# Third exp added ahead of the softmax sums, first adds on GpSimd, values and feed-forward one score burst later

## The chip, the cores and the metric

The kernel runs on one core of one Trainium2 chip. The metric is the device time of one execution in microseconds (us), as the median of several executions. Executions carry a state, fast or slow. All kernels of one group of runs ran on the same chip beside runs of the kernel before. A ratio below is the mean time of one kernel's fast runs over that of the kernel before's fast runs of the same rounds, so it is not quite the ratio of the medians that are quoted.

In this text TensorE is the matmul engine (PE in the profile, PEld its weight loads), VectorE is DVE, ScalarE is ACT, GpSimd is POOL.

## The reference

Grouped-query attention (batch 8, 16 query heads, 4 key and value heads, 384 positions, 64 wide), then a gated feed-forward with a spatial mix:

```python
scores = scale * q @ k.T ; attn = exp(scores - max) ; attn /= sum(attn) ; x = attn @ v
h = max(x @ w_in, 0) ; u, v = halves of h
v_n = (v - mean(v)) / sqrt(var(v) + 1e-6)
v_s = w_spatial @ v_n + b_spatial
out = (u * v_s) @ w_out
```

The kernel computes it per batch in f16 with f32 sums. It takes no maximum before the exp, which the size of the inputs allows.

## The kernel before: what matters

Every step is a small function, and a text lists the steps in the order in which they are issued. Each engine takes its own instructions from that text in that order; nothing overtakes on an engine. A step waits by semaphore for the data and buffers that it needs. A quote mark on a step means the batch before, two mean the one before that.

A batch has 18 score units: two groups of heads (gp), three chunks of 512 columns (c), three key tiles (t). The unit number u runs over t fastest. A "visit" is one burst of three units on TensorE (`s`), their three exps on ScalarE (`e`), and filler work for TensorE.

```python
def expo(b, u):      # ScalarE: aT[t] of 128x1024 f16 from two PSUM banks
    nc.scalar.activation(T["aT", b, gp][:, t, :, c*512:(c+1)*512], banks[...], AF.Exp, scale=scale)

def add(b, gp, c):   # "a": sT = aT[0] + aT[1], VectorE
    nc.vector.tensor_tensor(T["sT", b, gp][:, :, cs], aT[:, 0, :, cs], aT[:, 1, :, cs], ALU.add)

def add2(b, gp, c):  # "f": sT += aT[2]; in the file, but unused before
    T["all", b, gp] = True
    nc.vector.tensor_tensor(sT, sT, T["aT", b, gp][:, 2, :, cs], ALU.add)

def sums(b, gp, quad):  # "m": row sums by matmul with ones; one pass over each part
    parts = [aT[:, t] for t in range(NST)] if sT is None else [sT] if ("all", b, gp) in T else [sT, aT[:, 2]]
    tiles(f32(x, S), quad, [(ones32, a) for a in parts])
# "r": 1/sum by Ln and Exp on ScalarE; "x": values on TensorE; "n": xT = values * 1/sum on VectorE (PSUM in)
# "V": gate_v on TensorE and v_r = max(.,0) on VectorE; "S": bn_stats; "rs": rstd on ScalarE
def v_norm(b, engine):  # "vn": three of these, f32 in SBUF to f16 in SBUF
    engine.tensor_scalar(v_n, T["v_r", b, st], mv[:, st, 0:1], rstd[:, st:st+1], op0=ALU.subtract, op1=ALU.mult)
# "p": spatial, "U": gate_u, "O": project and an osb copy out of PSUM on VectorE ("Oc": in 32-column tiles)

C1 = "m10' m11' r10' r11' x100' n100' ... n111'"      # sums and values of group 1 of the batch before
C0 = "m00 m01 r00 r01 x000 n000 ... n011"
VISITS = [
    "s0 s1 s2 e0 e1 e2 a12' Oc0'' Oc1'' lk+ lq0+ lv+ lq1+", C1,
    "s3 s4 s5 e3 e4 e5 V0' S0' V1' S1' a00 a01 ck+ cq0+",
    "s6 s7 s8 e6 e7 e8 V2' S2' O2'' O3'' tk+ tq0+ cq1+ cv+",
    "s9 s10 s11 e9 rs' e10 e11 a02 Oc4'' Oc5'' vn' tq1+", C0,
    "s12 s13 s14 e12 e13 e14 p0' U0' p1' U1' a10",
    "s15 s16 s17 e15 e16 e17 p2' U2' p3' U3' a11",
]
```

The steps `ck cq cv` are casts of k, q and v on GpSimd. `banks` are the eight PSUM banks; a helper gives out the bank that was used longest ago. A score burst of three units takes six of them.

The softmax here doesn't subtract the row's maximum and nothing guards it: scores larger than these inputs give would overflow.

## Time and profile before

| | before |
|---|---|
| median of 3 runs | 256.83 us (256.55 to 256.88) |
| profiled span | 255.2 us |
| steady state | one batch every 28.8 us |

The page's first part gives each engine's busy time and share of the span:

```profile
PE 242.1 (95%) x2545; PEld 117.2 (46%) x2545; DVE 186.5 (73%) x348; ACT 172.1 (67%) x228; POOL 57.9 (23%) x100
```

TensorE is the busiest by far. A table of stretches shows one steady period. Its columns are the stretch, its length, then busy time of PE, PEld, DVE, ACT and POOL with their instruction counts, the granted TensorE clock, the DMA share and GB/s:

```profile
109.85:138.65 28.80, 28.43 (x307) 13.41 (x306) 22.24 (x40) 21.23 (x28) 6.85 (x10) 1.00 0.68 173
```

TensorE is busy 28.43 of 28.80 us at full clock. VectorE has 6.6 us to spare and GpSimd 22.

The timeline of another period (start, length, engine, line, operation; in brackets the idle time before it and what ended it) shows the work that the change removes, and a place where TensorE waits:

```profile
141.13 0.34 PE L331 MATMUL banks<-sT,ones 128*32 128x384 f16 x4
141.29 0.34 PE L331 MATMUL banks<-aT,ones 128*32 128x384 f16 x4
...
152.47 0.82 PE L309 MATMUL banks<-qT,kT 64*128 64x512 f16 x5
152.79 1.27 DVE L513 COPY osb<-banks 128x512 f32<-128x512 f32 x2
153.51 0.37 PE L309 MATMUL banks<-qT,kT 64*128 64x512 f16 x1 [0.22 <-DVE osb L513]
...
156.38 1.45 DVE L460 TENSOR_SCALAR v_n<-v_r,mv,rstd 128x512 f16<-128x512 f32 x3
```

The first two lines are the two-part sums. The next three show the last matmul of a score burst waiting for an osb copy to free its bank.

### The profile page before, as it was taken

The page shows a single profiled execution, that of the slowest core. Times are in us where ns is not written, and L with a number is a line of the kernel's source. Part 1 is how long each engine was busy: PE and PEld are TensorE (multiplying, and loading weights), DVE is VectorE, ACT ScalarE, POOL GpSimd, SP SyncE. Part 2 cuts the span into 40 slices and gives each one's busy share as a digit, 9 for nine tenths or more (in the row PEclk, how much of TensorE's full clock was granted, in tenths as well). Part 3 has the DMA queues.
Part 4 walks back from the last instruction along what each step waited for, and adds up shares of the span by engine and source line. Part 5 has one row for each costly group of instructions (what it writes and reads, how often), then busy time and mean ns, then how long its engine had stood idle before and what let it go on. Part 6 is the DMA issues. An engine that isn't in the chain of part 4 may idle for free.

```text
span 255.2 us, 6119 instructions
## 1 busy us (share of the span) xinstructions
PE 242.1 (95%) x2545; PEld 117.2 (46%) x2545; DVE 186.5 (73%) x348; ACT 172.1 (67%) x228; POOL 57.9 (23%) x100
## 2 busy tenths in 40 slices
PE   5899998979999999999999999999999999999993
PEld 5342434443454534553454434553354534554671
DVE  1544579987977599577976599577986599587953
ACT  3799799876766958776776958776776959730000
POOL 1717921624400054003700053002800000000000
PEclk9589999999999999999999999999999999999998
DMA  6999999959590688719591687519591204010424
GB/s 177 272 245 333 168 172 225 252 138 314 184 236 0 196 256 139 185 51 302 184 216 28 187 266 200 122 39 308 189 217 25 85 0 167 3 71 13 164 82 168
DMA packets 57228, 41.98 MB, mean 165 GB/s; under 512 B 26352, under 2 KB 53360, under 8 KB 57200
## 3 DMA queue, kind: packets, MB, share of 16 engines
q1 hardware_dynamic: 54208, 38.31, 55.9%
q0 software_dynamic: 2848, 3.15, 8.0%
q8 instruction: 20, 0.33, 0.5%
q10 hardware_dynamic: 144, 0.13, 0.1%
q14 instruction: 8, 0.07, 0.1%
HBM read 25.95 MB, written 12.58 MB: 151 GB/s over the span
## 4 chain that ended last, share of the span: by engine, by line
PE 57%; DVE 19%; DMA 12%; POOL 5%; SPq 3%; issue 3%; ACT 0%
PE banks L119 43%; DMA q<-in_q_dram 8%; PE banks L331 7%; PE banks L309 7%; DVE osb L513 4%; DVE sT L344 3%; DVE bn L449 3%; DVE v_n L460 3%; DVE v_r L436 3%; DVE xT L391 3%; DMA v<-in_v_dram 2%; POOL w_in L142 2%; DMA qT<-q 2%; POOL q L232 2%; SPq L210 1%
## 5 line engine op out<-in xcount | busy, mean ns | idle before, releaser
L321 ACT ACTIVATE aT<-banks 128x1024 f16<-128x1024 f32 x144 | 137.7, 1023 | 49.3 <-PE banks L309 48.4
L309 PE MATMUL banks<-qT,kT 64*128 64x512 f16 x288 | 47.0, 393 | 4.8 <-DMA qT<-q 1.5
L119 PE MATMUL banks<-xT,w_in 128*128 128x384 f16 (+1 forms) x320 | 47.2, 294 | 0.6 <-DVE v_r L438 0.6
L119 PE MATMUL banks<-w_out,gT 128*32 128x512 f16 (+2 forms) x508 | 45.4, 378 | 0.0
L119 PE MATMUL banks<-w_in,xT 128*128 128x512 f16 x192 | 44.7, 380 | 0.0
L391 DVE TENSOR_TENSOR xT<-banks,rec 128x384 f16<-128x384 f32 x64 | 31.4, 549 | 11.3 <-ACT rec L364 9.6
L232 POOL CAST q<-q 128x384 f16<-128x384 f32 x56 | 31.5, 594 | 16.2 <-DMA q<-in_q_dram 12.6
L119 PEld LDWEIGHTS <-w_in 128*128 128x128 f16 x320 | 27.3, 98 | 15.8 <-issue 1.4
L331 PE MATMUL banks<-aT,v 128*32 128x384 f16 x768 | 34.4, 326 | 0.0
L513 DVE COPY osb<-banks 128x512 f32<-128x512 f32 x47 | 31.2, 684 | 3.5 <-PE banks L119 3.4
L119 PEld LDWEIGHTS <-gT 128*32 128x32 f16 (+1 forms) x508 | 18.8, 96 | 27.1 <-issue 8.8
L189 POOL CAST k<-k 128x768 f16<-128x768 f32 x7 | 5.8, 829 | 104.2 <-DMA k<-in_k_dram 94.9
L119 PEld LDWEIGHTS <-xT 128*128 128x128 f16 x192 | 17.2, 98 | 25.6 <-issue 7.4
L344 DVE TENSOR_TENSOR sT<-aT 128x1024 f16<-128x1024 f16 x39 | 27.7, 738 | 0.0
L493 DVE SCALAR_TENSOR_TENSOR gT<-banks,vs 128x384 f16<-128x384 f32 x24 | 13.4, 558 | 17.0 <-PE banks L119 17.0
L331 PEld LDWEIGHTS <-v 128*32 128x32 f16 x768 | 20.3, 97 | 11.1 <-issue 0.8
L309 PEld LDWEIGHTS <-kT 64*128 64x128 f16 x288 | 11.2, 94 | 28.5 <-issue 22.3
L436 DVE TENSOR_SCALAR v_r<-banks 128x512 f32<-128x512 f32 x21 | 14.4, 688 | 11.8 <-PE banks L119 11.1
L119 PE MATMUL banks<-wsT,v_n 128*128 128x384 f16 x96 | 20.8, 327 | 0.8
L362 ACT ACTIVATE rec<-banks 128x384 f32<-128x384 f32 x32 | 15.6, 488 | 4.1 <-PE banks L331 4.0
L480 DVE TENSOR_TENSOR vs<-banks,bias_tp 128x384 f32<-128x384 f32 x28 | 15.6, 556 | 2.8 <-PE banks L119 2.8
L364 ACT ACTIVATE rec<-rec 128x384 f32<-128x384 f32 x32 | 16.7, 523 | 1.0
(49 smaller groups left out, 141.3 us busy)
## 6 DMA issues: line engine op xcount, KB each, us to landing
q<-in_q_dram SPq DMA_DIRECT2D x31, 384.0 KB, 6.9
out_dram<-osb SPq DMA_DIRECT2D x22, 512.0 KB, 3.2
v<-in_v_dram SPq DMA_DIRECT2D x8, 384.0 KB, 6.3
k<-in_k_dram SPq DMA_DIRECT2D x7, 384.0 KB, 5.7
w_in<-in_moe_w_in_dram POOLq DMA_DIRECT2D x16, 128.0 KB, 6.0
w_out<-in_moe_w_out_dram POOLq DMA_DIRECT2D x2, 512.0 KB, 9.3
out_dram<-osb SPq DMA_DIRECT2D x3, 256.0 KB, 2.0
ws<-in_moe_w_spatial_dram SPq DMA_DIRECT2D x1, 576.0 KB, 10.2
```

Of the source, the lines that this page charges most:

```text
L119: nc.tensor.matmul(dst[c : c + cols], w[:, c : c + cols], m, start=(i == 0), stop=(i == n - 1))
L232: engine(T["q16", b, gp][:, 2 * qd : 2 * qd + 2, :, half, :], T["q32", b, gp][:, qd, 2 * half : 2 * half + 2, :].rearrange("p j (t d) -> p ...
L309: nc.tensor.matmul(banks[:, xs[half], :], T["kT", b][lo:hi, t, gp, :], rhs[lo:hi, c * 512 : (c + 1) * 512], start=True, stop=True,)
L321: nc.scalar.activation(T["aT", b, gp][:, t, :, c * 512 : (c + 1) * 512], banks[:, x : y + 1 : y - x, :], AF.Exp, scale=scale)
L331: nc.tensor.matmul(dst[32 * i : 32 * (i + 1), :], weights if len(weights.shape) == 2 else weights[:, half, :], a[:, half, j * S : (j + 1) ...
L344: nc.vector.tensor_tensor(T["sT", b, gp][:, :, cs], aT[:, 0, :, cs], aT[:, 1, :, cs], ALU.add)
L362: nc.scalar.activation(rec, f32(x, S), AF.Ln)
L364: nc.scalar.activation(rec, rec, AF.Exp, scale=-1.0)
L391: nc.vector.tensor_tensor(T["xT", b][:, gp * 4 + quad * 2 + jj, :], f32(x, S), T["rec", b, gp, quad], ALU.mult)
L436: nc.vector.tensor_scalar(v_r, banks[:, x, :], 0.0, None, op0=ALU.max)
L480: nc.vector.tensor_tensor(vs, f32(x, S), bias_tp, ALU.add)
L513: copy(osb[:, half * 512 : (half + 1) * 512], banks[:, x, :])
```

## The change

Its intent: TensorE sets the period, so take matmuls from it. If the third exp is added too, each sum reads one part instead of two. The first add of each chunk goes to the idle GpSimd. Of the six second adds of a batch, which are new, five go to VectorE and one (`fp10`) to GpSimd. Since a GpSimd add takes longer, everything that depends on it moves one score burst later.

```diff
-    def add(b, gp, c):
+    def add(b, gp, c, engine=nc.vector):
...
-        nc.vector.tensor_tensor(T["sT", b, gp][:, :, cs], aT[:, 0, :, cs], aT[:, 1, :, cs], ALU.add)
+        engine.tensor_tensor(T["sT", b, gp][:, :, cs], aT[:, 0, :, cs], aT[:, 1, :, cs], ALU.add)
... (add2 in the same way)
+        "ap": lambda b, gp, c: add(b, gp, c, nc.gpsimd), "fp": lambda b, gp, c: add2(b, gp, c, nc.gpsimd),
...
     VISITS = [
-        "s0 s1 s2 e0 e1 e2 a12' Oc0'' Oc1'' lk+ lq0+ lv+ lq1+", C1,
-        "s3 s4 s5 e3 e4 e5 V0' S0' V1' S1' a00 a01 ck+ cq0+",
-        "s6 s7 s8 e6 e7 e8 V2' S2' O2'' O3'' tk+ tq0+ cq1+ cv+",
-        "s9 s10 s11 e9 rs' e10 e11 a02 Oc4'' Oc5'' vn' tq1+", C0,
-        "s12 s13 s14 e12 e13 e14 p0' U0' p1' U1' a10",
-        "s15 s16 s17 e15 e16 e17 p2' U2' p3' U3' a11",
+        "s0 s1 s2 e0 e1 e2 ap12' f12' p2'' U2'' p3'' U3'' lk+ lq0+ lv+ lq1+",
+        "s3 s4 s5 e3 e4 e5 Oc0'' Oc1'' ap00 f00 ck+ cq0+", C1,
+        "s6 s7 s8 e6 e7 e8 V0' S0' V1' S1' ap01 f01 tk+ tq0+ cq1+ cv+",
+        "s9 s10 s11 e9 e10 e11 V2' S2' rs' O2'' O3'' ap02 f02 vn' tq1+",
+        "s12 s13 s14 e12 e13 e14 Oc4'' Oc5'' ap10", C0,
+        "s15 s16 s17 e15 e16 e17 p0' U0' p1' U1' ap11 fp10 f11",
     ]
+    SUBS = "ap12' f12'=>a12';ap01=>a01;ap02=>a02;Oc0'' Oc1''=>Oc2'';p2'' U2'' p3'' U3''=>O0'' O1'';O2'' O3''=>O3''"
+    SECOND = STEADY with SUBS applied          # (written as a loop)
...
-            play(b, STEADY)
+            play(b, STEADY if b > 2 else SECOND)
```

The last part of the text (after the last batch) is changed to match. Batches 0 and 1 keep their old steps; batch 2, called SECOND, is the way into the new order.

More of the change, by code (lines that the diff above doesn't have):

```diff
@@ L343, in add, with add2 @@
         cs = slice(c * 512, (c + 1) * 512)
-        nc.vector.tensor_tensor(T["sT", b, gp][:, :, cs], aT[:, 0, :, cs], aT[:, 1, :, cs], ALU.add)
-    def add2(b, gp, c):
+        engine.tensor_tensor(T["sT", b, gp][:, :, cs], aT[:, 0, :, cs], aT[:, 1, :, cs], ALU.add)
+    def add2(b, gp, c, engine=nc.vector):
         T["all", b, gp] = True
@@ L349, in add2 @@
         sT = T["sT", b, gp][:, :, cs]
-        nc.vector.tensor_tensor(sT, sT, T["aT", b, gp][:, 2, :, cs], ALU.add)
+        engine.tensor_tensor(sT, sT, T["aT", b, gp][:, 2, :, cs], ALU.add)
     def sums(b, gp, quad):
@@ L580 @@
     STEPS = {
-        "w": idle, "s": score, "e": expo, "m": sums, "a": add, "f": add2, "r": recip, "rd": recip_v, "x": value, "n": norm,
+        "w": idle, "s": score, "e": expo, "m": sums, "a": add, "f": add2,
+        "ap": lambda b, gp, c: add(b, gp, c, nc.gpsimd), "fp": lambda b, gp, c: add2(b, gp, c, nc.gpsimd),
+        "r": recip, "rd": recip_v, "x": value, "n": norm,
         "V": gate_v, "S": stats, "rs": rstd, "vn": lambda b: v_norm(b, nc.vector),
@@ L640 @@
     VISITS = [
-        "s0 s1 s2 e0 e1 e2 a12' Oc0'' Oc1'' lk+ lq0+ lv+ lq1+", C1,
-        "s3 s4 s5 e3 e4 e5 V0' S0' V1' S1' a00 a01 ck+ cq0+",
-        "s6 s7 s8 e6 e7 e8 V2' S2' O2'' O3'' tk+ tq0+ cq1+ cv+",
-        "s9 s10 s11 e9 rs' e10 e11 a02 Oc4'' Oc5'' vn' tq1+", C0,
-        "s12 s13 s14 e12 e13 e14 p0' U0' p1' U1' a10",
-        "s15 s16 s17 e15 e16 e17 p2' U2' p3' U3' a11",
+        "s0 s1 s2 e0 e1 e2 ap12' f12' p2'' U2'' p3'' U3'' lk+ lq0+ lv+ lq1+",
[4 more added lines that the diff above has]
+        "s15 s16 s17 e15 e16 e17 p0' U0' p1' U1' ap11 fp10 f11",
     ]
     STEADY = " ".join(VISITS)
+    SUBS = "ap12' f12'=>a12';ap01=>a01;ap02=>a02;Oc0'' Oc1''=>Oc2'';p2'' U2'' p3'' U3''=>O0'' O1'';O2'' O3''=>O3''"
+    SECOND = STEADY
+    for x in SUBS.split(";"):
+        SECOND = SECOND.replace(*x.split("=>"), 1)
     FIRST = """lk+ lq0+ lv+ lq1+
@@ L655 @@
     LAST = """
-        a12' Oc0'' Oc1'' m10' m11' r10' r11' x100' n100' x101' n101' x110' n110' x111' n111'
-        V0' S0' V1' S1' V2' S2' O2'' O3'' rs' vn' O4'' O5''
+        ap12' f12' p2'' U2'' p3'' U3'' Oc0'' Oc1'' m10' m11' r10' r11' x100' n100' x101' n101' x110' n110' x111' n111'
+        V0' S0' V1' S1' V2' S2' Oa2'' rs' vn' O3'' O4'' O5''
         pz0' pz1' pz2' pz3' Uz0' Uz1' O0' O1' Uz2' Oh2' Oh3' Oh4' Oz5'"""
```

## The prediction

> **What bounds the kernel now.** The page gives TensorE 95% of the span, VectorE 73%, ScalarE 67%, GpSimd 23%. The chain of waits shows a steady state that repeats every 28.8 us (score bursts at 105.48, 134.28, 163.02, 191.81 us). The stretch view of such a period has TensorE busy 28.4 of 28.8 us, VectorE 22, ScalarE 21, GpSimd 6.8, granted clock 1.00. So TensorE's own instructions set the period. In the timeline two places of it run longer than their work: the score burst at 152.47 us takes 1.34 us instead of the usual 0.75 (its last matmul waits for a VectorE copy "osb"), and the burst at 158.25 takes 1.03 (the next weight load waits for v_n and norms behind VectorE). That is about 0.87 us per period. The chain runs through VectorE from 148 to 159 us: v_r, bn, two sT adds, osb, v_n, xT.
>
> **What the change removes.** Each chunk's sums now read one tile (sT of all three exps) instead of two. The instruction order shows 184 "ones" matmuls instead of 280: 96 fewer, in 24 groups of four concurrent ones. In the timeline 16 of them take 0.65 us to the next group, 0.1625 us a group: 24 x 0.1625 = 3.9 us, 0.65 us per batch, in batches 2 to 7. All of it lies on TensorE and so on the critical path.
>
> **What it adds and moves.** VectorE: six first adds per batch (0.66 us alone, mean 0.738) become five second adds of the same shape, so slightly less. GpSimd: seven adds of 128x1024 f16 per batch. No trace has one yet. The Trainium skill, "GPSIMD Engine Reference", section "Elementwise — side-by-side cycle accounting", gives about 2.6 cycles an element for two inputs at 1.2 GHz: estimate 2.2 us each, 15.5 us a period, with casts about 22 of 28. It fits, and each has nearly a whole visit (4 to 6 us) between its exps and its reader. The skill's "SBUF — State Buffer", section "Who interferes with whom", says that two-input VectorE operations and GpSimd reads block each other; the trace agrees: sT adds lie between 657 and 1312 ns, the long ones during casts, and casts stretch from 510 to 1034 ns. By my timing of the visits second adds mostly run when GpSimd has just finished; I allow 1 to 3 us of blocking per period, on VectorE, which has 6 us of slack.
> Moving the values and the feed-forward one burst later takes two adds out of the crowded v_r stretch and moves v_n a burst ahead of its reader. I expect this to win back about 0.5 of the 0.87 us stall per period, 2.3 us over five periods. The ramp before 52 us is unchanged; the tail keeps its TensorE order and gains some tenths.
>
> **Prediction.** 256.8 - 3.9 - 2.3 + 0.3 for new waits: 250.9 us, eight in ten between 248.5 and 254.3. Faster by over 2%: 0.60; within 2%: 0.35; slower by over 2%: 0.05.
>
> **What would show it.** Period near 27.7 us; "ones" matmul busy about 7 us lower; GpSimd adds of 2.0 to 2.6 us and GpSimd busy near 150 us; no burst of over 1.1 us in steady state; VectorE second adds of 0.66 to 1.5 us.
>
> **What would make it wrong.** GpSimd adds of over 3 us: GpSimd then bounds the period, VectorE stands behind a late first add, and evacuations, banks and score bursts wait. Long mutual blocking: second adds of 2 us and more. Casts held behind adds, so transposes of q and k land after their burst. Or the stall only moves to another burst: then about 253 us.

## More of the kernel before

Experiments 1 to 4, 5 to 8 and 9 to 10 ran on three different chips; the kernel before had medians of 256.71, 256.73 and 256.88 us there.

From the table of groups (line, engine, operation, output and inputs, count, then total busy us and mean ns of one):

```profile
L344 DVE TENSOR_TENSOR sT<-aT 128x1024 f16<-128x1024 f16 x39 | 27.7, 738 | 0.0
L331 PE MATMUL banks<-aT,ones 128*32 128x384 f16 x176 | 12.6, 332 | 0.0
L460 DVE TENSOR_SCALAR v_n<-v_r,mv,rstd 128x512 f16<-128x512 f32 x24 | 12.2, 562 | 0.0
L331 PE MATMUL banks<-sT,ones 128*32 128x384 f16 x104 | 8.6, 326 | 0.0
```

## The result, and the profile after

| | before | after |
|---|---|---|
| median | 256.69 us (4 runs) | 272.51 us (271.0 to 273.61, 4 runs) |
| ratio of fast runs | | 1.0615, 95% interval 1.0561 to 1.0668 |
| profiled span | 255.2 us | 270.5 us |
| steady period | 28.8 us | 30.4 us |

The result is correct and slower by 6%. The page, the stretch of one period, and the groups that answer to those above:

```profile
PE 244.2 (90%) x2437; PEld 117.8 (44%) x2437; DVE 202.3 (75%) x343; ACT 172.5 (64%) x229; POOL 141.1 (52%) x140
```

```profile
115.61:146.08 30.47, 28.54 (x289) 13.32 (x290) 24.15 (x39) 21.14 (x28) 20.66 (x17) 1.00 0.64 164
```

```profile
L344 POOL TENSOR_TENSOR sT<-aT 128x1024 f16<-128x1024 f16 x34 | 73.2, 2153 | 62.1 <-ACT aT L321 62.1
L350 DVE TENSOR_TENSOR sT<-sT,aT 128x1024 f16<-128x1024 f16 x30 | 28.4, 962 | 0.1
L460 DVE TENSOR_SCALAR v_n<-v_r,mv,rstd 128x512 f16<-128x512 f32 x24 | 22.7, 1003 | 0.6 <-ACT rstd L455 0.6
L331 PE MATMUL banks<-sT,ones 128*32 128x384 f16 x104 | 7.3, 342 | 3.4 <-DVE sT L350 3.4
L331 PE MATMUL banks<-aT,ones 128*32 128x384 f16 x80 | 5.0, 349 | 0.0
```

The work did go away: 184 matmuls with "ones" instead of 280. The GpSimd adds took 2.15 us, the estimate was 2.2. What is new is on VectorE. v_n has a mean of 1003 ns instead of 562 although not a bit of it was changed, and the second adds have 962. VectorE is busy 24.15 us a period instead of 22.24, with one add fewer.

The timeline of a period shows where. A first place, the second add of chunk 0 (L350):

```profile
122.77 2.15 POOL L344 TENSOR_TENSOR sT<-aT 128x1024 f16<-128x1024 f16 x1
123.37 2.10 DVE L350 TENSOR_TENSOR sT<-sT,aT 128x1024 f16<-128x1024 f16 x1
125.39 1.94 DVE L391 TENSOR_TENSOR xT<-banks,rec 128x384 f16<-128x384 f32 x4
125.99 0.84 PE L309 MATMUL banks<-qT,kT 64*128 64x512 f16 x2 [0.47 <-DVE xT L391]
```

GpSimd starts its next first add at 122.77, VectorE starts its second add at 123.37, and that ends at 125.47, just after GpSimd's end at 124.92. It takes 2.10 us instead of 0.68. The four norms (L391) come behind it, and TensorE's score burst waits for the bank of a norm. Burst and wait take 2.0 us, from 124.92 to 126.92, instead of 0.75.

The second place is v_n. In narrow windows of the timeline the third of the three stands alone:

```profile
137.26 2.22 POOL L344 TENSOR_TENSOR sT<-aT 128x1024 f16<-128x1024 f16 x1 [2.17 <-ACT aT L321]
137.41 2.36 DVE L460 TENSOR_SCALAR v_n<-v_r,mv,rstd 128x512 f16<-128x512 f32 x1
...
139.69 1.28 DVE L513 COPY osb<-banks 128x512 f32<-128x512 f32 x2
140.89 1.94 DVE L391 TENSOR_TENSOR xT<-banks,rec 128x384 f16<-128x384 f32 x4
141.02 1.30 PE L309 MATMUL banks<-qT,kT 64*128 64x512 f16 x6 [1.10 <-DVE osb L513]
```

The third v_n begins 0.15 us after a GpSimd add and ends 0.29 us after its end: 2.36 us for an operation of 0.54. Two osb copies stand behind it, and TensorE sits idle 1.10 us for the bank of the second.

Against 0.66 and 0.54 us alone, VectorE loses 1.44 + 1.82 = 3.3 us per period in these two places. The period is 1.7 us longer instead of 1.1 shorter.

The periods are only half of the loss. Counting score matmuls (36 per batch) gives the time of each batch's first burst: batch 2 begins at 52.41 us before and 50.30 after, batch 3 at 81.06 and 85.21, batch 7 at 196.18 and 207.02. The new order puts 3.7 us of TensorE work (p2 U2 p3 U3) from batch 2 off to the end, so batch 2 should have been 3.7 us shorter. Instead it is 6.3 us longer. The balance of the 15.3 us between the spans is then: the ramp -2.1, batch 2 about +9.9, the four periods of batches 3 to 6 +6.7, batch 7 and the tail +0.8.

The ramp is the same code in both; TensorE waits there for a transpose of q by DMA, 1.47 us in this run of the kernel before and not at all in this one of the kernel after (2.0 and 3.7 us in two runs below). I take it as chance.

The stretches of batch 2 after (columns as above) show a second effect on top of the waits:

```profile
54.00:56.00 2.00, 0.10 (x2) 0.09 (x1) 2.00 (x2) 2.00 (x3) 1.21 (x1) 1.00 0.00 0
56.00:58.00 2.00, 1.58 (x16) 0.69 (x19) 0.96 (x2) 0.56 (x1) 0.00 (x0) 0.57 0.08 31
...
74.00:76.00 2.00, 0.23 (x8) 0.18 (x11) 2.00 (x2) 0.71 (x2) 2.00 (x2) 1.00 0.80 147
78.00:80.00 2.00, 1.66 (x17) 0.59 (x10) 2.00 (x4) 0.00 (x0) 0.00 (x0) 0.50 0.00 0
```

TensorE is nearly idle from 54 to 56 us and from 72 to 76 us (its longest single waits are 2.32 and 3.39 us). Then the granted clock is 0.50 for 3.41 us, from 56.28 and from 76.76 us, and 1.00 before and after; the stretches of 2 us above show it as 0.57 and 0.50. The Trainium skill, "TensorE: Matmul & The Clock Gate", section "Part 1: The HAM clock gate (the "warmup" mystery)", says that after an idle window of about 3.4 us the clock goes to half, and returns after about 3.4 us of work. This trace agrees with half the clock, 0.50, and with its length, 3.41 us; on the length of the idle time see the last section.

### The profile page after: what moved, and what is told of

The parts are those of the page before. It is cut to its first block, busy times and chain, and to the rows that moved or that the text cites. A ratio compares the mean times of both kernels' runs of the same rounds, so it can differ in the third digit from the quotient of the medians.

```text
span 270.5 us, 5961 instructions
## 1 busy us (share of the span) xinstructions
PE 244.2 (90%) x2437; PEld 117.8 (44%) x2437; DVE 202.3 (75%) x343; ACT 172.5 (64%) x229; POOL 141.1 (52%) x140
## 4 chain that ended last, share of the span: by engine, by line
PE 70%; DVE 19%; ACT 4%; issue 2%; DMA 2%; SPq 0%; POOL 0%; DVEq 0%
PE banks L119 51%; PE banks L331 11%; PE banks L309 9%; DVE xT L391 7%; DVE osb L513 3%; ACT aT L321 3%; DVE sT L344 2%; DMA q<-in_q_dram 1%; DVE sT L350 1%; DVE bn L449 1%; DVE v_n L460 1%; DMA out_dram<-osb 1%; DVE v_r L438 1%; ACT rec L364 1%; DVE v_r L436 0%
## 5 line engine op out<-in xcount | busy, mean ns | idle before, releaser
L344 POOL TENSOR_TENSOR sT<-aT 128x1024 f16<-128x1024 f16 x34 | 73.2, 2153 | 62.1 <-ACT aT L321 62.1
L309 PE MATMUL banks<-qT,kT 64*128 64x512 f16 x288 | 49.5, 380 | 12.8 <-DVE osb L513 5.8
L119 PE MATMUL banks<-w_out,gT 128*32 128x512 f16 (+2 forms) x496 | 46.7, 386 | 2.5 <-DVE osb L513 2.3
L513 DVE COPY osb<-banks 128x512 f32<-128x512 f32 x46 | 30.3, 682 | 9.7 <-PE banks L119 9.7
L391 DVE TENSOR_TENSOR xT<-banks,rec 128x384 f16<-128x384 f32 x64 | 31.3, 544 | 8.1 <-ACT rec L364 5.7
L331 PE MATMUL banks<-aT,v 128*32 128x384 f16 x768 | 35.7, 334 | 0.0
L232 POOL CAST q<-q 128x384 f16<-128x384 f32 x56 | 29.3, 562 | 10.4 <-DMA q<-in_q_dram 8.7
L119 PEld LDWEIGHTS <-w_in 128*128 128x128 f16 x320 | 27.3, 98 | 15.8 <-issue 1.4
L309 PEld LDWEIGHTS <-kT 64*128 64x128 f16 x288 | 12.9, 94 | 39.7 <-issue 33.6
L350 DVE TENSOR_TENSOR sT<-sT,aT 128x1024 f16<-128x1024 f16 x30 | 28.4, 962 | 0.1
L331 PEld LDWEIGHTS <-v 128*32 128x32 f16 x768 | 21.1, 99 | 11.6 <-issue 0.7
L460 DVE TENSOR_SCALAR v_n<-v_r,mv,rstd 128x512 f16<-128x512 f32 x24 | 22.7, 1003 | 0.6 <-ACT rstd L455 0.6
```

The costliest lines, as they stand in the source:

```text
L119: nc.tensor.matmul(dst[c : c + cols], w[:, c : c + cols], m, start=(i == 0), stop=(i == n - 1))
L232: engine(T["q16", b, gp][:, 2 * qd : 2 * qd + 2, :, half, :], T["q32", b, gp][:, qd, 2 * half : 2 * half + 2, :].rearrange("p j (t d) -> p ...
L309: nc.tensor.matmul(banks[:, xs[half], :], T["kT", b][lo:hi, t, gp, :], rhs[lo:hi, c * 512 : (c + 1) * 512], start=True, stop=True,)
L331: nc.tensor.matmul(dst[32 * i : 32 * (i + 1), :], weights if len(weights.shape) == 2 else weights[:, half, :], a[:, half, j * S : (j + 1) ...
L344: engine.tensor_tensor(T["sT", b, gp][:, :, cs], aT[:, 0, :, cs], aT[:, 1, :, cs], ALU.add)
L350: engine.tensor_tensor(sT, sT, T["aT", b, gp][:, 2, :, cs], ALU.add)
```

## The experiments

The theory (port): a GpSimd add holds something that VectorE's two-input adds and v_n need, for its whole 2.15 us; VectorE waits in order, and TensorE waits behind it for banks and norms. Rivals: the new order itself is worse, whoever adds (order); the first adds come too late out of GpSimd's queue, and VectorE waits for their data (lateness).

### 1. No first adds at all

Its output is wrong, which doesn't matter for the time. The order of everything else stays.

```diff
-  "ap": lambda b, gp, c: add(b, gp, c, nc.gpsimd), "fp": lambda b, gp, c: add2(b, gp, c, nc.gpsimd),
+  "ap": lambda b, gp, c: skipped.add((b, gp, c)), "fp": lambda b, gp, c: add2(b, gp, c),
...
-        engine.tensor_tensor(sT, sT, T["aT", b, gp][:, 2, :, cs], ALU.add)
+        first = aT[:, 0, :, cs] if (b, gp, c) in skipped else sT
+        engine.tensor_tensor(sT, first, aT[:, 2, :, cs], ALU.add)
```

> The changed kernel with every add on GpSimd taken away (wrong result on purpose: the sums miss the middle third; the one add on GpSimd that is a second add goes to VectorE). TensorE's order is unchanged. Port theory (an add on GpSimd shuts out VectorE's two-input adds and v_n for its whole 2.15 us): no v_n or sT operation on VectorE above 1.1 us, the two stalls per period vanish, period about 27.6 us instead of 30.4, time 248 to 252 us. Order theory (values and feed-forward one burst later is itself the worse order, by banks and ScalarE): period stays at 30 us or so, time above 266 us.

Measured: 252.59 us (ratio 0.9854, 0.9805 to 0.9902). One period (stretch view):

```profile
108.67:136.27 27.60, 27.50 (x289) 12.92 (x288) 21.68 (x40) 21.14 (x28) 5.91 (x10) 1.00 0.72 180
```

27.60 us. The v_n mean is 539 ns. The time is 0.6 us above the expected range. The order theory falls: in the new order, without GpSimd's adds, the period is 1.2 us shorter than before. This period also agrees with two terms of the prediction together, 0.65 us of sums and 0.5 us of former stalls. The first can be read by itself: before, a set of sums takes 0.65 us up to the first matmul with values (from 141.13 us), in the changed kernel 0.33 (from 122.53 us), and a period has two sets. The second is what is left.

### 2. All adds on VectorE

```diff
-  "ap": lambda b, gp, c: add(b, gp, c, nc.gpsimd), "fp": lambda b, gp, c: add2(b, gp, c, nc.gpsimd),
+  "ap": add, "fp": add2,
```

> The changed kernel with all twelve adds of a batch on VectorE, none on GpSimd; correct result. VectorE gets 7 adds of 0.66 us back, about 4.6 us per period, and would be busy some 25.5 us of a period; so it is no free gain. Port theory: v_n back to 0.54 us each and adds to 0.66 to 0.9, period 28 to 29 us, time 252 to 260 us, faster than the changed kernel although VectorE has more work. Order theory: slower than the changed kernel (over 272 us), since VectorE only gets more to do.

Measured: 269.68 us (ratio 1.0509, 1.0479 to 1.0538), correct. v_n is back at 556 ns and the adds at 0.73 and 0.77 us, as expected, and it is faster than the changed kernel. But the time is far outside the range, with a period of 30.97 us and VectorE busy 26.3 of it. Its trace shows that at the start of a batch five adds in a row (4.3 us, the second adds of the last visit among them) stand ahead of the evacuations of p2 and U2, so the next score burst waits for banks twice. So GpSimd was not the worst choice; VectorE has room on average but not in that place. I had judged from the sum.

### 3. Batch 2 with plain adds

```diff
+    for x in "ap00 f00=>a00;a01 f01=>a01;a02 f02=>a02;ap10=>a10;ap11 fp10 f11=>a11".split(";"):
+        SECOND = SECOND.replace(*x.split("=>"), 1)
...
-            play(b, STEADY if b > 2 else SECOND)
+            play(b, STEADY if b > 3 else STEADY.replace("ap12' f12'", "a12'") if b > 2 else SECOND)
```

> The changed kernel with batch 2 alone (the first in the new order) back to first adds only, on VectorE, so with no add on GpSimd and two-part sums in that batch. By my count of the marks the first batch in the new order costs about 10 us of the 15, and the later periods 1.65 us each. Port theory: this batch gets about 8 us shorter, time about 264 us (262 to 267), the later periods stay at 30.4 us. If the transition is slow for its order (casts and loads of k late, copies in the wrong place), the time moves by less than 3 us.

Measured: 265.10 us (ratio 1.0319, 1.0290 to 1.0349), correct. Batch 2 goes from 34.9 to 26.5 us, the later periods stay at 30.4 us. So nearly half of the loss (7.4 of 15.8 us by the medians) lay in one batch of eight, and went with its GpSimd adds. The edit takes away second adds of that batch as well, so it doesn't by itself say which of the two mattered.

### 4. Two second adds earlier in VectorE's order

```diff
-        "s3 s4 s5 e3 e4 e5 Oc0'' Oc1'' ap00 f00 ck+ cq0+", C1,
+        "s3 s4 s5 e3 e4 e5 ap00 f00 Oc0'' Oc1'' ck+ cq0+", C1,
...
-        "s9 s10 s11 e9 e10 e11 V2' S2' rs' O2'' O3'' ap02 f02 vn' tq1+",
+        "s9 s10 s11 e9 e10 e11 ap02 f02 V2' S2' rs' O2'' O3'' vn' tq1+",
```

> The changed kernel with two second adds earlier in VectorE's order, nothing else: f of chunk 0 ahead of the two osb copies, f of chunk 2 ahead of the third v_r. GpSimd does the same adds. Port theory: these adds and v_n then start when no GpSimd add is running, so the f of chunk 0 goes from 2.1 to below 1.2 us, the third v_n from 2.36 to 0.54, the period from 30.4 to about 28 us in the five periods, time about 261 us (258 to 265). Lateness theory (VectorE stands because the first adds come late out of GpSimd's queue): second adds moved forward wait for them, period same or longer, time 271 or more.

Measured: 255.14 us over all runs (four fast ones of 253.11 to 255.50; ratio 0.9934, 0.9906 to 0.9963), correct. The profile fell in a slow run of 257.76 us, so I use only its period, 27.74 us. Timeline:

```profile
116.72 0.93 DVE L350 TENSOR_TENSOR sT<-sT,aT 128x1024 f16<-128x1024 f16 x1
...
131.06 1.45 DVE L460 TENSOR_SCALAR v_n<-v_r,mv,rstd 128x512 f16<-128x512 f32 x3
132.42 2.13 POOL L344 TENSOR_TENSOR sT<-aT 128x1024 f16<-128x1024 f16 x1 [2.03 <-ACT aT L321]
```

The second add of chunk 0 now takes 0.93 us (it starts beside casts), and the three v_n 1.45 us: they end 0.1 us after the GpSimd add begins, not after it ends. The same instructions, two of them in another place, gave 17 us back. I had expected some 11; the two moved adds also sit in batch 2. The lateness theory falls: adds that were late would not gain by being asked for earlier.

### 5. Both edits

```diff
  the edits of experiments 3 and 4 together
```

> The earlier order of the two second adds together with the plain batch 2 (first adds only, on VectorE, in that batch). Both edits act on different stretches, so their gains should add: period 27.7 us, batch 2 about 26.5 us, time 255.1 - 6 = 249 us (247.5 to 251.5), faster than the kernel before by over 2%. If the loss of batch 2 was in part the same as that of the periods (a lag carried forward), it is 252 or more.

Measured: 251.60 us (four fast runs of 251.45 to 252.21; ratio 0.9797, 0.9750 to 0.9845), correct. This is 0.1 us above the range, and whether it is over 2% faster stays unclear. Against the mean of the fast runs of experiment 4 (254.5 us) plain batch 2 brought about 3 us, not 6. I had taken the 6 from the profile of experiment 4, which fell in a slow run, as this one's did; that was a mistake of method, and no profile of a fast run shows where the difference lies.

### 6. GpSimd held back

VectorE's order is that of the changed kernel. GpSimd alone waits, by a one-column copy that reads what VectorE must have finished.

```diff
+    def guard(column):
+        nc.gpsimd.tensor_copy(scratch, column)
...
-        "s6 s7 s8 e6 e7 e8 V0' S0' V1' S1' ap01 f01 tk+ tq0+ cq1+ cv+",
+        "s6 s7 s8 e6 e7 e8 V0' S0' V1' S1' gf00 ap01 f01 tk+ tq0+ cq1+ cv+",   # gf00: guard(last column of f00's output)
...
-        "s15 s16 s17 e15 e16 e17 p0' U0' p1' U1' ap11 fp10 f11",
+        "s15 s16 s17 e15 e16 e17 p0' U0' p1' U1' gv' ap11 fp10 f11",           # gv': guard(last column of the third v_n)
```

> The changed kernel with VectorE's order untouched; GpSimd alone is held: a one-column copy on GpSimd of the output of f of chunk 0 ahead of its next first add, and of the third v_n ahead of the first add of chunk 1 of the second group, so GpSimd starts these two adds up to 1 us later than it could. Port theory: the f of chunk 0 goes from 2.1 to 0.7 us, the third v_n from 2.36 to 0.54, the period from 30.4 to 27.6-28 us, time 253 to 259 us: a slower start of GpSimd makes the kernel faster. Lateness theory: first adds come still later, period 30.4 or more, time 271 or more. Order theory: no change, 271.

Measured: 253.88 us (ratio 0.9897, 0.9848 to 0.9946), correct. Timeline of a period:

```profile
117.41 0.68 DVE L350 TENSOR_TENSOR sT<-sT,aT 128x1024 f16<-128x1024 f16 x1
118.30 2.13 POOL L344 TENSOR_TENSOR sT<-aT 128x1024 f16<-128x1024 f16 x1
...
129.47 1.46 DVE L465 TENSOR_SCALAR v_n<-v_r,mv,rstd 128x512 f16<-128x512 f32 x3
131.20 2.13 POOL L344 TENSOR_TENSOR sT<-aT 128x1024 f16<-128x1024 f16 x1
```

The add takes 0.68 us and the three v_n 1.46 us, each with the GpSimd add behind it. The period is 27.61 us, the same as with no first adds at all (27.60). So these two collisions account for the whole loss of the steady state, and a GpSimd that starts later makes the kernel 18.6 us faster by the medians (batch 2 gains too: 31.2 us).

### 7. GpSimd adds in halves

```diff
+        for h in [slice(0, 1), slice(1, 2)] if engine is nc.gpsimd else [slice(0, 2)]:
-        engine.tensor_tensor(T["sT", b, gp][:, :, cs], aT[:, 0, :, cs], aT[:, 1, :, cs], ALU.add)
+            engine.tensor_tensor(T["sT", b, gp][:, h, cs], aT[:, 0, h, cs], aT[:, 1, h, cs], ALU.add)
... (add2 in the same way)
```

> The changed kernel with each GpSimd add cut into two of 512 columns. Port theory (VectorE waits for the end of the one GpSimd instruction that is running): the longest v_n and f fall from 2.4 to about 1.3 us, period about 28.5 to 29.3 us, time 259 to 266 us. If VectorE only gets the port when GpSimd's queue is empty, or if the two share bandwidth, the longest stay at 2.0 us and more and the time stays near 272.

Measured: 261.45 us (ratio 1.0177, 1.0121 to 1.0233), correct, period 28.64 us. By tile, minimum, median and maximum in ns:

```profile
L462 DVE TENSOR_SCALAR v_n<-v_r,mv,rstd x24: 530/543/1384, 41.9 to 243.1; 128x512 f16<-128x512 f32 x24
L345 POOL TENSOR_TENSOR sT<-aT x68: 1140/1154/1607, 53.8 to 225.3; 128x512 f16<-128x512 f16 x68
L352 DVE TENSOR_TENSOR sT<-sT,aT x30: 657/683/1455, 58.2 to 228.0; 128x1024 f16<-128x1024 f16 x30
```

The longest v_n falls from 2366 to 1384 ns and the longest second add from 2423 to 1455. VectorE's wait is the rest of the one GpSimd instruction that is running; it gets its turn between two of them.

### 8. The collision by itself

A probe behind the last work of the kernel before. Each VectorE operation is issued after a filler (bn_stats), beside a GpSimd operation or none.

```diff
+        for g in ("none", "add", "cast", "fill"):
+            for v in ("two", "vn", "psum", "bn"):
+                o = gps(g, ...)                      # GpSimd: nothing, add 128x1024 f16, cast 128x768, fill 128x2048 f16
+                nc.vector.bn_stats(pbn, pv)          # the filler
+                ... the VectorE operation v, then a wait for both
```

> The kernel before, with a probe after its last work: each of four VectorE operations (two-input add of 128x1024 f16; v_n's form; the norm's form with one input in PSUM; bn_stats) is issued about 0.7 us after a GpSimd operation has begun (none; two-input add 128x1024 f16; cast 128x768 f32 to f16; fill of 128x2048 f16). Port theory: beside the GpSimd add the two-input add and v_n end only after it (1.5 to 2.2 us instead of 0.66 and 0.54); norm and bn_stats keep 0.55 and 0.7 us. Beside a cast the same with a shorter wait. Beside a fill, which reads nothing: if only the read side is shared by a two-input add, that add keeps 0.66 us, while v_n may wait. If GpSimd slows VectorE in general, the norm and bn_stats grow too.

Timeline:

```profile
254.79 0.67 DVE L701 TENSOR_TENSOR d_none_two<-pa,pb 128x1024 f16<-128x1024 f16 x1
256.11 0.53 DVE L703 TENSOR_SCALAR d_none_vn<-pv,pm 128x512 f16<-128x512 f32 x1
...
259.15 2.12 POOL L688 TENSOR_TENSOR g_add_two<-pa,pb 128x1024 f16<-128x1024 f16 x1 [75.19 <-DVE pw L714]
259.48 2.33 DVE L701 TENSOR_TENSOR d_add_two<-pa,pb 128x1024 f16<-128x1024 f16 x1
...
262.46 2.04 DVE L703 TENSOR_SCALAR d_add_vn<-pv,pm 128x512 f16<-128x512 f32 x1
265.31 0.54 DVE L705 TENSOR_TENSOR d_add_psum<-banks,pr 128x384 f16<-128x384 f32 x1
...
275.91 0.68 DVE L701 TENSOR_TENSOR d_fill_two<-pa,pb 128x1024 f16<-128x1024 f16 x1
276.77 1.81 POOL L692 MEMSET g_fill_vn<- 128x2048 f16 x1
277.57 1.29 DVE L703 TENSOR_SCALAR d_fill_vn<-pv,pm 128x512 f16<-128x512 f32 x1
```

In us, VectorE's operation by what ran on GpSimd:

| VectorE operation | alone | beside add (2.12) | beside cast (0.83) | beside fill (1.81) |
|---|---|---|---|---|
| add, two inputs in SBUF | 0.67 | 2.33 | 1.01 | 0.68 |
| v_n, f32 to f16 in SBUF | 0.53 | 2.04 | 0.72 | 1.29 |
| norm, one input in PSUM | 0.54 | 0.54 | 0.54 | 0.54 |
| bn_stats, one input | 0.68 | 0.68 | 0.68 | 0.68 |

Each cell is one operation in one execution. The two operations began 0.33 to 0.39 us apart beside the add and the cast, not 0.7, and the add's 2.33 us lies above the expected 1.5 to 2.2. Both that grow end 0.3 to 0.6 us after the GpSimd operation's end. The Trainium skill, "SBUF — State Buffer", section "Who interferes with whom", says just this: a two-input VectorE instruction contends with a GpSimd instruction that reads SBUF and not with one that only writes; VectorE's two-port modes contend with any; the loser blocks for the whole instruction; one SBUF input outside those modes does not contend. Every cell of the table agrees, if v_n runs in a two-port mode, which no run here shows by itself. That the fill spares the add and holds v_n also excludes that GpSimd slows VectorE in general.

### 9. Held GpSimd and plain batch 2

```diff
  the edits of experiments 3 and 6 together (batch 2 without its holds)
```

> The two holds on GpSimd (which gave a period of 27.61 us) with the plain batch 2 (first adds only, on VectorE). Batch 2 took 31.2 us with the holds alone and 26.5 us in the plain form of an earlier run, so up to 4.7 us less than the 253.9 us of the holds alone: 249 to 250.5 us, ratio to before 0.970 to 0.977. If the gain of the plain batch 2 is as small as in the combination with the earlier order (3.5 us), it is 250.4. It would beat both kernels.

Measured: 250.08 us (249.85 to 250.79, 6 runs; ratio 0.9751, 0.9727 to 0.9775), correct. It beats both kernels, the one before by 2.5% and the changed one by 22 us. Its stretch view:

```profile
81.20:108.80 27.60, 27.60 (x298) 13.06 (x296) 20.90 (x39) 21.13 (x28) 20.02 (x19) 1.00 0.67 175
```

TensorE is busy through the whole stretch. Batch 2 takes 26.05 us at a clock of 1.00.

### 10. Second adds in the old order

```diff
  (the kernel before, its VISITS with an f for each a, on VectorE; f01 stands one visit after a01)
-        "s3 s4 s5 e3 e4 e5 V0' S0' V1' S1' a00 a01 ck+ cq0+",
+        "s3 s4 s5 e3 e4 e5 V0' S0' V1' S1' a00 f00 a01 ck+ cq0+",
...
```

> The kernel before in its own order, with a second add on VectorE after each first add in batches 2 to 7 (from the last chunk of batch 2 on in the next visit); no add on GpSimd, nothing moved. TensorE loses the same 24 groups of sums, 0.65 us per period, but VectorE gets six adds of 0.66 us more where it was crowded (22 of 28.8 us busy). If TensorE's work alone set the period: 28.1 us and 252.8 us. If the VectorE stretch around v_r, bn and v_n sets it in part, as the chain of the kernel before says: period 28.8 to 30.5 us, 256 to 265 us. I expect the second; it would show that the move to GpSimd or in the order is needed for the gain.

Measured: 272.86 us (ratio 1.0653, 1.0602 to 1.0704), correct; batches 2 to 6 take 30.6, 31.5, 32.4, 32.4 and 31.3 us. The direction was as expected, the size not: 16 us instead of at most 8. Stretches of one of the two longest:

```profile
162.40:165.30 2.90, 1.15 (x7) 0.30 (x6) 2.83 (x6) 2.38 (x4) 2.45 (x5) 1.00 0.06 17
165.30:168.70 3.40, 3.40 (x33) 1.28 (x36) 2.57 (x4) 1.02 (x1) 0.66 (x1) 0.51 1.05 185
```

VectorE is full in the first stretch and TensorE idles 1.75 us for an osb copy; then the granted clock is 0.51 for 3.4 us. The clock falls in the two batches of 32.4 us alone; a wait of the same 1.75 us, up to 197.47 us, left it at 1.00. So it costs such a batch about 1 us, an estimate from 32.4 against 31.3 to 31.5 us, and the rest of the loss against 28.8 us is there without it: TensorE waits 1.3 to 2.0 us for that osb copy in every batch. So in the old order and without GpSimd the 0.65 us of saved sums buy nothing. With experiment 2, neither order has room for all the adds on VectorE; the versions that gained have the first adds on GpSimd, or none, in the new order.

## Why the prediction was wrong

It said 250.9 us, faster; it was 272.51, slower by 6%.

- TensorE sets the period, and 24 groups of sums at 0.1625 us go away: right. The matmul count is 184, and the group lines of the "ones" matmuls fall from 12.6 + 8.6 to 5.0 + 7.3 us. That is 8.9 us lower; I had said about 7.
- GpSimd adds of 2.2 us, busy near 150: right. 2153 and 2350 ns, 141.1 us busy. The skill's "GPSIMD Engine Reference", section "3.1 Elementwise — side-by-side cycle accounting", was a good source for this.
- Of the signs that it named, those of the amounts of work came as said and those of the waiting did not: the period was 30.4 us and not 27.7, second adds reached 2.42 us and not 1.5, and a steady burst took 2.0 us and not under 1.1.
- The move wins back about 0.5 us of stalls per period: right as to the order alone, taken together with the sums. With GpSimd's adds away or held, periods are 27.60 and 27.61 us, against 28.8 - 0.65 - 0.5 = 27.65.
- The step that failed: "By my timing of the visits second adds mostly run when GpSimd has just finished; I allow 1 to 3 us of blocking per period, on VectorE, which has 6 us of slack." The blocking was 3.3 us per period, little above the range. What was wrong is that slack in the sum would take it up. The block fell on the add in front of the norms and on the v_n in front of the osb copies, where TensorE waits for the very next VectorE operation. Experiment 4 moved two second adds, experiment 6 held GpSimd until these two operations were done; neither collided with a GpSimd add any more, and the periods were 27.74 and 27.61 us.
- A second part of that step: I worked out the timing of second adds and did not do it for v_n, though the page that I used says that two-port modes contend too. v_n lost more (1.8 us) than the add (1.4 us).
- Not costed at all: batch 2. I read the steady text and took the way into it as free. It cost 9.9 of the 15.3 us: three VectorE adds (2.19 to 2.61 us each) and a v_n waited for GpSimd adds there, TensorE starved twice, and its clock fell after each time. An estimate puts at most 3.2 us of it to the clock: TensorE was busy 3.27 and 3.05 us in the two stretches of 3.41 us at half clock, and at full clock that work would take half as long.
- What I had named as a way to be wrong, "Long mutual blocking: second adds of 2 us and more", is what happened, for one VectorE second add in five (and for v_n); I gave slower by over 2% only 0.05.

How much of batch 2's loss came from each collision is not settled; experiments 3 and 6 show 26.5 and 31.2 us against 34.9, and no run took its collisions away one by one.

## What to carry to other kernels

Before work goes to GpSimd, list VectorE's instructions with two SBUF inputs and its SBUF-to-SBUF ones like v_n, and check for each in the timeline whether a GpSimd instruction will be running when it starts; the cost is about the rest of that instruction (1.44 and 1.82 us here), paid by whatever stands behind on VectorE. If it collides, change who starts first: move the VectorE operation, hold GpSimd by a small data dependence, or cut the GpSimd instruction. Slack in a period's sum is no slack at a place where the bounding engine waits for the next instruction, and the way into a new steady state has to be costed like the steady state itself.

## What the Trainium skill lacked or had wrong

- "TensorE: Matmul & The Clock Gate" puts the fall of the clock after an idle window of about 3.4 us and advises no gaps above about 3 us. Here shorter ones were enough at times: 2.32 us idle in batch 2 of the changed kernel was followed by 3.41 us at 0.50, and 1.75 us idle, ended by one matmul, by 3.4 us at 0.51 (experiment 10). At other times they were not: in experiment 10 a wait of 2.65 us, up to 53.65 us, and one of 1.75 us, up to 197.47 us, left the clock at 1.00, as did the 1.10 us gaps of the changed kernel's steady periods. So in these runs the length of one gap does not by itself say whether the clock falls.
- "SBUF — State Buffer", "Who interferes with whom", was contradicted by none of the twelve cells of the probe with a GpSimd operation, and by no other run. What it lacks is the size of the penalty at the end for a VectorE operation that waits for GpSimd: VectorE's operation ended 0.54 us after the GpSimd add for the two-input add and 0.27 us after it for v_n, so most of the add's own 0.67 us and half of v_n's 0.53 still come after the wait.
- "GPSIMD Engine Reference" has no figure for f16 two-input adds: 2.12 us for 128x1024 alone, 1.15 us for 128x512 (experiment 7), so a half costs 54% of the whole.
